# Five blocks of small products move into another PSUM pool, each directly beside a second set of small products

## The chip, the cores and the metric

The kernel runs on one core of a Trainium2 chip. The metric is the device time of one execution in microseconds. Five engines work side by side: PE (TensorE, matrix products), DVE (VectorE), ACT (ScalarE), POOL and SP (both used here to issue DMAs). Each engine takes its instructions strictly in the order in which the program was written; between engines, semaphores hold an instruction back until what it needs is there.

## The reference

Two branches over 2048 tokens of 512 channels are mixed by a gate for each token:

```python
g = sigmoid((x * gate_w).sum(-1, keepdims=True))
# branch a: a diagonal state space model as a long convolution
dt = exp(log_dt); A = -exp(log_A_real) + 1j * A_imag; C = (C_real + 1j * C_imag) * dt[:, None]
P = exp((A * dt[:, None])[:, :, None] * arange(2048))     # (512, 128, 2048)
K = 2.0 * einsum("dn,dnl->dl", C, P).real
a = irfft(rfft(u, 4096) * rfft(K, 4096))[:2048] + u * D_skip
# branch b: a bilinear gated unit, 512 -> 1792 -> 512
b = einsum("bsf,fd->bsd", (x @ w_gate) * (x @ w_up), w_down)
out = g * a + (1 - g) * b
```

## The kernel before

**Branch b** is most of PE's work. F = 1792 is cut into 14 slices, handled in four groups (3, 3, 4 and 4); for each group the four chunks of 512 tokens are gone through. `hidden` makes the products with the gate and the up weights in two PSUM banks, `pg` and `pu`, one bank each; `down` makes the products with the down weights in banks called `y`, of which there are two. To keep float32 accuracy with the fast float32r products, every operand is split into a high and a low part, and each product is three matmuls of 128x128 by 128x512 (called a *triple* below: `pg<-xs,wlo` once and `pg<-xs,whi` twice, or `y<-dhi,hl`, `y<-dlo,hh`, `y<-dhi,hh`). ACT copies `pg` to `h`, DVE multiplies `h` by `pu`, ACT and DVE split the result into `hh` and `hl`; ACT scales a finished `y` into `acc`, which is added to the output by a DMA.

**Branch a** makes the convolution kernel K in 16 blocks of 32 channels (`k_block(b, ...)`, b = 0 to 15). DVE and ACT build two tables of powers, `x` and `v`, and PE multiplies them: 64 small matmuls (128 rows by 32 columns of the array, 64 elements each) into one PSUM bank, `pk`. One ACT copy and two DVE operations take the bank into the tile `kt`. The transforms of u and of K, their products and the way back are further *sets of small products*, of other shapes, which take tiles of 32 or 64 rows of the array: `k<-in,w2s`, `k<-kt,w1k_t`, `k<-y,w3s`, `k<-in,w_t`. In the profile these small float32 products show as two records each. All of them, and `pk`, take banks called `k`, of which there are four (`bank()`). So PSUM's eight banks are: `y` two, `pg` and `pu` one each, `k` four.

**The order.** Every operation is first recorded as a task with an engine, a duration, and the tiles that it reads and writes (`Work.add`). `Work.plan` sorts the tasks with a model of the five engines, of the DMAs and of PE's instruction stream, and `Work.run` then writes them out in that order, after some of them have been moved by hand: a pair (n, other) in the table `AHEAD` puts task n directly before task other. This written order is the order on every engine. A PSUM or SBUF tile gets its buffer in the same order, in turn, and waits for the readers of the tile that had the buffer before.

On PE the sets of small products stand one at a time between the triples of branch b. All instructions are recorded through the helper class `InOrder`, so all carry one line in the profile (L124); tiles tell them apart.

Of the kernel before, what the change touches and what calls it, by code (L numbers as in the profile page):

```python
# [23 lines left out]
GROUPS = [range(0, 3), range(3, 6), range(6, 10), range(10, 14)]  # L24
SLOTS = max(map(len, GROUPS))
LAST = 3 if len(GROUPS) % 2 else 0
ROUND = 1.5 * 2.0**23
LN2_HI = 355.0 / 512.0
LN2_LO = math.log(2.0) - LN2_HI
# [86 lines left out]
class InOrder:  # L116


    def __init__(self, tc, engine):
        self.tc, self.engine, self.last = tc, engine, None  # L120
# [49 lines left out]
class Bus:  # L170
# [25 lines left out]
    def add(self, task, at, us):  # L196
        at = max(at, self.now)
        self.serve(self.queues, self.now, at)
        self.now = at
        self.queues[task.engine == "pool"].append([task, us])  # L200
        self.loads.append((at, sum(x[1] for q in self.queues for x in q)))
        return self.serve([[[*x] for x in q] for q in self.queues], at, 1e9)


class Work:
# [39 lines left out]
    SURE = {"pe": 3, "act": 2, "dve": 2}  # L245

    def __init__(self):
        self.tags, self.tasks = {}, []

    def tile(self, pool, tag, shape, dtype=F32, bufs=1, loose=False):  # L250
        return Tile(self, pool, tag, shape, dtype, bufs, loose)
# [189 lines left out]
            order.append(t)  # L441
        return order

    AHEAD = ((250, 57), (293, 292), (365, 364), (437, 436), (1140, 2246), (1149, 2246))

    def run(self):
        order = self.plan()
        at = {t.n: t for t in order}
        for n, other in self.AHEAD:
            order.remove(at[n])  # L450
            order.insert(order.index(at[other]), at[n])
            assert all(order.index(d) < order.index(at[n]) for d in at[n].deps)
        for t in order:
            t.fn()

# [2 lines left out]
def gated_mix_kernel(  # L458
# [19 lines left out]
    work = Work()  # L478
# [3 lines left out]
    def open_pool(name, bufs=1, space=None):  # L482
        kw = {} if space is None else {"space": space}
        return ctx.enter_context(tc.tile_pool(name=name, bufs=bufs, **kw))
# [9 lines left out]
    pools = {n: open_pool(n, b, PSUM) for n, b in (("ps_y", 2), ("ps_g", 1), ("ps_k", 4))}  # L494
# [3 lines left out]
    def new(pool, tag, shape, dtype=F32, bufs=1, loose=False):  # L498
        return work.tile(pools[pool], tag, shape, dtype, bufs, loose)

    def bank():
        return new("ps_k", "k", [P, D], bufs=4, loose=True)
# [5 lines left out]
    def stage(shape):  # L508
        return new("mid", "ts", shape, bufs=2, loose=True)
# [18 lines left out]
    def memsets():  # L528
        dve.memset(half_pi, math.pi / 2)
        dve.memset(shift, ROUND)  # L530
        dve.memset(skip, 0.0)
# [198 lines left out]
    def evacuate(gi, ci, r, y):  # L730
        t = 4 * ci + r
        final = gi == len(GROUPS) - 1 and ci == LAST
        if final and r > 1:
# [17 lines left out]
    def ends():  # L751

        t0 = 4 * LAST
        sums = new("tab", "kt", [P, 4, D])
# [4 lines left out]
        for r, acc in ending:  # L759
            t = t0 + r  # L760
            for q, (fin, parts) in late["fin"].items():
                add(
                    "dve", 0.25,
                    lambda r=r, q=q, t=t, fin=fin: dve.scalar_tensor_tensor(
                        sums.t[:, r, P * q : P * q + P], fin.t[:, 4 * (LAST % 2) + r], gate[:, t : t + 1],
                        sums.t[:, r, P * q : P * q + P], op0=ALU.mult, op1=ALU.add,
                    ),
                    r=[*parts, (m_gate, LAST)], w=[(sums, (r, 1))], rank=0,
                )
            for n, cs in enumerate((slice(0, D // 2), slice(D // 2, D)) if r == 3 else (slice(0, D),)):  # L770
# [7 lines left out]

                add("dve", 0.42 if r == 3 else 0.69, total, r=[acc, (m_gate, LAST)], w=part, rank=0)
                e, q = ("act", act) if n else ("sp", sp)  # L780
# [122 lines left out]
    def prologue():  # L903
# [23 lines left out]
        def exp(us, src, er, en, ep, ei, r, w, after=0.0):  # L927
# [9 lines left out]
            def ts(o, i, a, b, op0, op1=None):  # L937
                kw = {"op0": op0} if op1 is None else {"op0": op0, "op1": op1}
                op(0.62, "tensor_scalar", lambda: ((o(), i(), a, b), kw))

            def stt(o, i, a, j, op0, op1):
                op(1.0, "scalar_tensor_tensor", lambda: ((o(), i(), a, j()), {"op0": op0, "op1": op1}))

            ts(er, src, -87.0, 88.0, ALU.max, ALU.min)
            ts(en, er, 1.0 / math.log(2.0), ROUND, ALU.mult, ALU.add)
            ts(en, en, ROUND, None, ALU.subtract)
            stt(er, en, -LN2_HI, er, ALU.mult, ALU.add)
# [80 lines left out]
    def phases(b):  # L1028
# [7 lines left out]
            "dve", 0.85,  # L1036
            lambda: dve.scalar_tensor_tensor(t.t, rt.t, ROUND, t.t, op0=ALU.subtract, op1=ALU.subtract),
            r=[rt], w=[t],
# [132 lines left out]

    def k_block(b, x, v):
        pk = bank()

        def kgen():
            pv = pk.t.rearrange("p (g j) -> p g j", j=64)
            for g in range(TB // 4):
                for c in range(2):
                    for ch in range(4):
                        d = 4 * g + ch  # L1180
                        pe.matmul(
                            pv[32 * ch : 32 * ch + 32, g, :], x.t[:, c, d, :], v.t[:, c, d, :], start=c == 0, stop=c == 1,
                            tile_position=(0, 32 * ch),
                        )

        if b % 4 == 0:
            kts["now"] = new("tab", "kt", [P, 2, 2, 32, 16])
        kt, g0 = kts["now"], b % 4 * 8
        add("pe", 2.05, kgen, r=[x, v], w=[pk], rank=0, hold=[kt], count=256, slack=1.0)
        pv = lambda a: pk.t.rearrange("p (g a b k) -> p g a b k", a=2, b=2, k=16)[:, :, a]  # L1190
        side = lambda h: kt.t[:, h, :, g0 : g0 + 8].rearrange("p b g k -> p g b k")
        add("act", 0.37, lambda: act.copy(side(1), pv(0)[:, :, :, ::-1]), r=[pk], w=[(kt, (1, b % 4))])
        for h, op in enumerate((ALU.add, ALU.subtract)):
            add(
                "dve", 0.42, lambda h=h, op=op: dve.tensor_tensor(out=side(h), in0=pv(1), in1=side(1), op=op),
                r=[pk, (kt, (1, b % 4))], w=[(kt, (h, b % 4))], rank=0,
            )
        if b % 4 == 3:
            k_first(b // 4, kt)
# [196 lines left out]
    def m_last(q, gs):  # L1396

        banks, pieces, src = [[bank() for _ in range(2)] for _ in gs], [], []
        for g in gs:
# [6 lines left out]
            src.append(t)  # L1406
            cuts = ((1 - LAST % 2, 1), (LAST % 2, 1)) if q >= KT - 2 and g == LAST // 2 else ((0, 2),)
            to = t if q >= KT - 2 else stage([P, 8, P])
# [104 lines left out]
    for b in range(NB):  # L1513
        if b + 1 < NB:
            if b % 2 == 0:
                amplitudes([n for n in (b + 1, b + 2) if n < NB])
            phases(b + 1)
        v, old = v_table(b), x
        if b + 1 < NB:
            direct_powers(b + 1)  # L1520
            leads(b + 1)
            x = x_table(b + 1)
        k_block(b, old, v)
        if b % 4 == 3:
            transforms(b // 4)
# [56 lines left out]
```

## Time and profile before

| | |
|---|---|
| median of 3 runs | 579.96 us (579.47 to 580.79) |
| the profiled execution | 580.89 us |
| its span, from first to last instruction | 579.1 us |
| around the span | 1.8 us |
| PE, DVE, ACT, POOL busy in the span | 99%, 88%, 69%, 20% |
| DMA | 136.28 MB, mean 235 GB/s |
| granted TensorE clock | 1.0 in the whole span |

The profile is of one execution. Busy times are sums over the span, and a matmul's end is modelled, since matmuls overlap: the distance from one start to the next is the time that a matmul takes on PE. "PEld" are the weight loads that go with the matmuls. The queue "q8 instruction" among the DMA queues carries instruction code.

### The profile page before, as it was taken

The page shows a single profiled execution, that of the slowest core. Times are in us where ns is not written, and L with a number is a line of the kernel's source. Part 1 is how long each engine was busy: PE and PEld are TensorE (multiplying, and loading weights), DVE is VectorE, ACT ScalarE, POOL GpSimd, SP SyncE. Part 2 cuts the span into 40 slices and gives each one's busy share as a digit, 9 for nine tenths or more (in the row PEclk, how much of TensorE's full clock was granted, in tenths as well). Part 3 has the DMA queues.
Part 4 walks back from the last instruction along what each step waited for, and adds up shares of the span by engine and source line. Part 5 has one row for each costly group of instructions (what it writes and reads, how often), then busy time and mean ns, then how long its engine had stood idle before and what let it go on. Part 6 is the DMA issues. An engine that isn't in the chain of part 4 may idle for free.

```text
span 579.1 us, 14843 instructions
## 1 busy us (share of the span) xinstructions
PE 573.0 (99%) x5998; PEld 433.5 (75%) x5998; DVE 510.4 (88%) x812; ACT 401.4 (69%) x891; POOL 113.4 (20%) x159
## 2 busy tenths in 40 slices
PE   9999999999999999999999999999999999999997
PEld 5777777888886777788677868876778786776775
DVE  6999999999998999999999999997999996247555
ACT  5459888997579499968896775799887544243351
POOL 0003222312010240311032401103332103111011
PEclk9999999999999999999999999999999999999999
DMA  8999969998565797989679848978989349798986
GB/s 283 403 360 362 412 217 351 279 215 241 119 182 154 260 244 174 252 196 293 191 218 264 181 129 251 224 181 211 306 132 289 72 154 277 235 307 222 277 168 127
DMA packets 71687, 136.28 MB, mean 235 GB/s; under 512 B 6852, under 2 KB 35780, under 8 KB 69188
## 3 DMA queue, kind: packets, MB, share of 16 engines
q1 hardware_dynamic: 47668, 87.10, 43.3%
q0 software_dynamic: 23392, 47.98, 39.6%
q8 instruction: 47, 0.77, 0.5%
q10 hardware_dynamic: 560, 0.26, 0.2%
q14 instruction: 20, 0.16, 0.1%
HBM read 80.27 MB, written 55.05 MB: 234 GB/s over the span
## 4 chain that ended last, share of the span: by engine, by line
PE 94%; DMA 3%; ACT 1%; DVE 1%; issue 1%; DVEq 0%
PE pg L124 26%; PE y L124 26%; PE pu L124 26%; PE k L124 16%; DMA raw<-in_wts 2%; DMA y<-in_xT 1%; ACT ev L124 0%; ACT acc L124 0%; DVE dlo L124 0%; DVE t L124 0%; DVE v L124 0%; DVE sq L124 0%; ACT xs L124 0%; ACT v L124 0%; ACT h L124 0%
## 5 line engine op out<-in xcount | busy, mean ns | idle before, releaser
L124 PE MATMUL pg<-xs,whi 128*128 128x512 f32 x448 | 138.7, 391 | 0.2 <-ACT whi L124 0.2
L124 PE MATMUL pu<-xs,whi 128*128 128x512 f32 x448 | 138.3, 390 | 0.0
L124 PEld LDWEIGHTS pg<-xs,whi 128*128 128x128 f32 x448 | 84.1, 188 | 18.1 <-DVE xs L124 0.6
L124 PEld LDWEIGHTS pu<-xs,whi 128*128 128x128 f32 x448 | 84.1, 188 | 17.0
L124 PE MATMUL y<-dhi,hl 128*128 128x512 f32 x224 | 90.2, 403 | 0.1
L124 PE MATMUL pg<-xs,wlo 128*128 128x512 f32 x224 | 89.7, 400 | 0.5 <-ACT h L124 0.4
L124 PE MATMUL pu<-xs,wlo 128*128 128x512 f32 x224 | 89.4, 399 | 0.2 <-issue 0.2
L124 PE MATMUL y<-dlo,hh 128*128 128x512 f32 x224 | 87.7, 391 | 0.0
L124 PE MATMUL y<-dhi,hh 128*128 128x512 f32 x224 | 87.2, 389 | 0.0
L124 POOL DMA_DIRECT2D out<-acc x44 | 38.5, 929 | 171.0 <-ACT acc L124 170.4
L124 ACT COPY ev<-k 128x512 f32<-128x512 f32 x112 | 59.3, 598 | 14.8 <-PE k L124 12.3
L124 ACT CAST hh<-h 128x512 fp32r<-128x512 f32 x56 | 34.7, 620 | 44.6 <-DVE h L124 44.3
L124 DVE TENSOR_TENSOR h<-pu,h 128x512 f32<-128x512 f32 x56 | 38.5, 688 | 25.1 <-PE pu L124 22.5
L124 ACT ACTIVATE acc<-y,ngate 128x512 f32<-128x512 f32 x62 | 42.0, 688 | 24.3 <-PE y L124 22.8
L124 PEld LDWEIGHTS y<-dhi,hl 128*128 128x128 f32 x224 | 42.0, 188 | 21.0 <-issue 8.3
L124 PEld LDWEIGHTS pg<-xs,wlo 128*128 128x128 f32 x224 | 42.0, 188 | 20.1 <-issue 10.1
L124 PEld LDWEIGHTS pu<-xs,wlo 128*128 128x128 f32 x224 | 42.0, 188 | 17.2 <-issue 7.6
L124 ACT COPY h<-pg 128x512 f32<-128x512 f32 x56 | 33.0, 588 | 29.3 <-PE pg L124 24.6
L124 PEld LDWEIGHTS y<-dhi,hh 128*128 128x128 f32 x224 | 42.1, 188 | 9.0
L124 PEld LDWEIGHTS y<-dlo,hh 128*128 128x128 f32 x224 | 42.1, 188 | 8.1 <-issue 0.3
L124 DVE TENSOR_TENSOR hl<-h,hh 128x512 fp32r<-128x512 f32 x56 | 38.4, 687 | 3.6 <-ACT hh L124 3.1
L124 DVE TENSOR_TENSOR v<-m,v 128x896 f32<-128x896 f32 x32 | 34.1, 1085 | 0.2
(130 smaller groups left out, 959.2 us busy)
## 6 DMA issues: line engine op xcount, KB each, us to landing
xs<-xs_d SPq DMA_DIRECT2D x36, 512.0 KB, 6.0
out<-acc POOLq DMA_DIRECT2D x44, 256.0 KB, 6.0
raw<-in_wts SPq DMA_DIRECT2D x33, 256.0 KB, 4.8
xs_d<-xs SPq DMA_DIRECT2D x16, 512.0 KB, 7.8
su_d<-ev POOLq DMA_DIRECT2D x32, 256.0 KB, 6.1
y_d<-ts SPq DMA_DIRECT2D x28, 256.0 KB, 5.6
in<-su_d POOLq DMA_DIRECT2D x12, 512.0 KB, 7.2
sk_d<-ev SPq DMA_DIRECT2D x6, 1024.0 KB, 3.8
```

What stands on the lines that cost most here:

```text
L124: got = getattr(self.engine, name)(*args, **kw)
```

## The change

Five of the sixteen K blocks (0, 5, 8, 14 and 15) get their PSUM bank from the pool of the two `y` banks instead of the four `k` banks. The tile is planned as before, and takes its new home only when the order stands (`work.moved`). The table `AHEAD` grows, so that on PE each of these blocks stands directly beside another set of small products, with no triple between them; a few operations of ACT and DVE are moved with them. No operation is added or removed, and the orders on SP and POOL stay as they were.

```diff
+BESIDE = 0, 5, 8, 14, 15
...
-        self.tags, self.tasks = {}, []
+        self.tags, self.tasks, self.moved = {}, [], []
...
-    AHEAD = ((250, 57), (293, 292), (365, 364), (437, 436), (1140, 2246), (1149, 2246))
+    AHEAD = (
+        (250, 57), (293, 292), (365, 364), (437, 436),
+        (444, 167), (1485, 445), (170, 451), (171, 451), (1490, 451),
...
+    )
...
-            assert all(order.index(d) < order.index(at[n]) for d in at[n].deps)
+        self.checked(order)
+        for tile, home in self.moved:
+            tile.pool, tile.tag, tile.bufs = home
         for t in order:
             t.fn()
...
     def k_block(b, x, v):
         pk = bank()
+        if b in BESIDE:
+            work.moved.append((pk, (pools["ps_y"], "y", 2)))
```

(`checked` goes through the order and asserts that every task stands behind those that it depends on.)

On PE, around K block 0, before the change (the names carry buffer numbers; `k_1155<-in` is the last of a set of the first transform of u, `k_1193<-v` the K block, `pg` and `pu` are triples):

```order
L124 MATMUL k_1155<-in_875,w2s_164 64x512
L124 MATMUL pg_1143<-xs_944,wlo_214 128x512
L124 MATMUL pg_1143<-xs_944,whi_204 128x512 x2
L124 MATMUL pg_1143<-xs_950,wlo_214 128x512
L124 MATMUL pg_1143<-xs_950,whi_204 128x512 x2
L124 MATMUL pg_1143<-xs_1055,wlo_214 128x512
L124 MATMUL pg_1143<-xs_1055,whi_204 128x512 x2
L124 MATMUL k_1193<-v_752,x_458 32x64 x64
L124 MATMUL pu_1273<-xs_679,wlo_214 128x512
```

And after it:

```order
L126 MATMUL pg_1143<-xs_944,whi_204 128x512 x2
L126 MATMUL k_1152<-in_875,w2s_164 64x512
L126 MATMUL k_1154<-in_875,w2s_164 64x512
L126 MATMUL k_1156<-in_875,w2s_164 64x512
L126 MATMUL k_1158<-in_875,w2s_164 64x512
L126 MATMUL y_1176<-v_752,x_458 32x64 x64
L126 MATMUL pg_1143<-xs_950,wlo_214 128x512
L126 MATMUL pg_1143<-xs_950,whi_204 128x512 x2
L126 MATMUL pg_1143<-xs_1055,wlo_214 128x512
L126 MATMUL pg_1143<-xs_1055,whi_204 128x512 x2
L126 MATMUL pu_1273<-xs_679,wlo_214 128x512
```

The set of the transform stands one triple later, and the K block two triples earlier, now in a `y` bank. K blocks 5 and 8 come to stand behind such a set in the same way (two triples and six triples earlier), and block 14 keeps its place while the set behind it comes three triples earlier.

On PE, around K block 15, before the change (`k_6278<-v` is the K block; the set `k_6225` to `k_6231` that will stand beside it is four triples ahead):

```order
L124 MATMUL y_6205<-dhi_5447,hl_6185 128x512
L124 MATMUL y_6205<-dlo_5468,hh_6183 128x512
L124 MATMUL y_6205<-dhi_5447,hh_6183 128x512
L124 MATMUL pg_6265<-xs_5656,wlo_4868 128x512
L124 MATMUL pg_6265<-xs_5656,whi_4850 128x512 x2
L124 MATMUL y_6272<-dhi_5281,hl_5891 128x512
L124 MATMUL y_6272<-dlo_5294,hh_5882 128x512
L124 MATMUL y_6272<-dhi_5281,hh_5882 128x512
L124 MATMUL k_6278<-v_752,x_5763 32x64 x64
```

And after it (`y_6272` is now the K block's bank, `y_6337` the sums that were `y_6272`):

```order
L126 MATMUL pg_6231<-xs_5656,whi_4850 128x512 x2
L126 MATMUL k_6235<-in_5593,w2s_5591 32x512
L126 MATMUL k_6237<-in_5593,w2s_5591 32x512
L126 MATMUL k_6239<-in_5593,w2s_5591 32x512
L126 MATMUL k_6241<-in_5593,w2s_5591 32x512
L126 MATMUL y_6272<-v_752,x_5763 32x64 x64
L126 MATMUL y_6337<-dhi_5281,hl_5891 128x512
```

The set moved three triples later, the K block one triple earlier, and the K block takes a `y` bank in turn between two pairs of sums.

On ACT, where K block 12 is taken out of its bank (it keeps a `k` bank), before the change (`ts` is scaled by the gate in two halves, `dhi<-raw` is the high part of down weights that a DMA brings, `h<-pg` empties the bank `pg`):

```order
L124 ACTIVATE ts_5267<-ts_5267,gate_83 128x128 x8
L124 ACTIVATE ts_5276<-ts_5276,gate_83 128x128 x8
L124 CAST dhi_5433<-raw_5303 128x512
L124 CAST hh_5439<-h_5322 128x512
L124 COPY x_5445<-pb_4184 128x64
L124 CAST dhi_5447<-raw_5309 128x512
L124 COPY kt_5455<-k_5324 128x8x2x16
L124 COPY h_5459<-pg_5423 128x512
```

And after it:

```order
L126 ACTIVATE ts_5267<-ts_5267,gate_83 128x128 x8
L126 COPY kt_5411<-k_5324 128x8x2x16
L126 ACTIVATE ts_5276<-ts_5276,gate_83 128x128 x8
L126 CAST dhi_5437<-raw_5303 128x512
L126 CAST hh_5443<-h_5322 128x512
L126 COPY x_5451<-pb_4184 128x64
L126 COPY h_5453<-pg_5425 128x512
L126 CAST dhi_5455<-raw_5309 128x512
```

The copy of the K block comes ahead of eight operations of the scaling, and the second `dhi<-raw` stands behind `h<-pg` instead of ahead of it.

More of the change, by code (lines that the diff above doesn't have):

```diff
@@ L442, in plan, with checked @@
         return order
-    AHEAD = ((250, 57), (293, 292), (365, 364), (437, 436), (1140, 2246), (1149, 2246))
+    AHEAD = (
[8 rows of a table added]
+    )
+    @staticmethod
+    def checked(order):
+        done = set()
+        for t in order:
+            assert t.deps <= done
+            done.add(t)
     def run(self):
```

6 rows, old and new, of the table AHEAD are left out of this document.

## The prediction

> **What bounds the kernel now.** I read the page first (busy shares, chain, queues), then PE's waits, then PE's timeline at the five places, then DVE and ACT there, and last the fetches of instruction code. The page:
>
> ```profile
> span 579.1 us, 14843 instructions
> ...
> PE 573.0 (99%) x5998; PEld 433.5 (75%) x5998; DVE 510.4 (88%) x812; ACT 401.4 (69%) x891; POOL 113.4 (20%) x159
> ...
> q8 instruction: 47, 0.77, 0.5%
> ...
> PE 94%; DMA 3%; ACT 1%; DVE 1%; issue 1%; DVEq 0%
> ```
>
> PE is busy 99% of the span and carries 94% of the chain that ended last. PE's waits hold little, and these two are the ones far inside the span (at 420 and at 382):
>
> ```profile
> PE pg L124 <- ACT h L124: 0.4, 1, 0.4
> ...
> PE pu L124 <- issue: 0.2, 1, 0.2
> ```
>
> So what PE saves is saved, and what holds PE is lost, nearly everywhere. The busy share hides what a set of small products costs beside its own work. The timeline of PE around K block 5 (start, duration, engine, instruction, count) shows it:
>
> ```profile
> 215.63 0.39 PE L124 MATMUL pu<-xs,wlo 128*128 128x512 f32 x1
> ...
> 216.40 1.14 PE L124 MATMUL k<-in,w2s 32*32 32x512 f32 x32
> 217.47 0.50 PE L124 MATMUL pu<-xs,wlo 128*128 128x512 f32 x1
> ...
> 218.27 0.40 PE L124 MATMUL pg<-xs,wlo 128*128 128x512 f32 x1
> ...
> 218.96 0.39 PE L124 MATMUL pg<-xs,wlo 128*128 128x512 f32 x1
> ...
> 219.73 1.99 PE L124 MATMUL k<-v,x 128*32 128x64 f32 x128
> 221.66 0.50 PE L124 MATMUL pg<-xs,wlo 128*128 128x512 f32 x1
> ...
> 222.46 0.40 PE L124 MATMUL pg<-xs,wlo 128*128 128x512 f32 x1
> ```
>
> A triple takes 0.68 (three starts 0.227 apart). After the triple at 215.63 the next start would be 216.31; the set comes at 216.40, 0.09 late. The triple behind the set lasts 217.47 to 218.27, 0.80, 0.12 over. The K set pays the same: 218.96 + 0.68 = 219.64 against 219.73, and 221.66 to 222.46. A visit to small products so costs 0.21 us beside its work.
>
> **The change, part by part.** *Five visits fewer.* Two sets side by side pay one entry and one return instead of two. No trace row shows two sets of different shapes meeting. If PE passes from one to the other as it now passes to a triple, 0.21 is saved; if the meeting costs another entry, 0.12; if the second set slips in without the 0.09, 0.30. I take 0.21, since entry (0.09) and the wait at a set's end look alike for all shapes of set here. The Trainium skill, "TensorEngine Tiling (Array Packing)", Key Properties, says that changing the tiling mode drains the array; no run here shows it between two small modes; by it the end 0.30 falls away.
>
> *Inputs and banks.* A K block that moves forward needs `x` and `v` sooner. At block 0 the last write of `v` on DVE, and PE's timeline:
>
> ```profile
> 95.89 0.66 DVE L124 TENSOR_TENSOR v<-v,sq 128x256 f32<-128x256 f32 x1
> ```
>
> ```profile
> 94.54 0.39 PE L124 MATMUL pg<-xs,wlo 128*128 128x512 f32 x1
> ...
> 95.31 1.11 PE L124 MATMUL k<-in,w2s 32*64 32x512 f32 x16
> 96.35 0.50 PE L124 MATMUL pg<-xs,wlo 128*128 128x512 f32 x1
> ...
> 98.61 2.17 PE L124 MATMUL k<-v,x 128*32 128x64 f32 x128
> 100.72 0.50 PE L124 MATMUL pu<-xs,wlo 128*128 128x512 f32 x1
> ```
>
> The set now starts a triple later, 95.99, and takes 96.35 - 95.31 = 1.04, so block 0 starts at 97.03, 0.5 after `v` (96.55). Block 15 has the least room (PE, DVE, ACT):
>
> ```profile
> 478.45 1.14 PE L124 MATMUL k<-in,w2s 32*32 32x512 f32 x32
> ...
> 482.46 1.99 PE L124 MATMUL k<-v,x 128*32 128x64 f32 x128
> ```
>
> ```profile
> 480.18 0.62 DVE L124 TENSOR_TENSOR v<-v,sq 128x256 f32<-128x256 f32 x1
> ```
>
> ```profile
> 480.52 1.38 ACT L124 ACTIVATE acc<-y,ngate 128x512 f32<-128x512 f32 x2
> ```
>
> Block 15 starts a triple and the set's saved 0.21 + 0.12 earlier, near 481.4 to 481.6; `v` is written at 480.80, and the `y` bank that it takes is emptied by the first of two `acc` at about 481.2, or 0.5 sooner since one `ev` copy no longer stands ahead of it. Its own bank is wanted again by the second pair of sums, 12 matmuls or 2.72 after its end, while the copy and the two DVE operations follow within 2. I cost this at nothing; if the cover fails, PE waits some 0.3 there. At the other four places the next `y` comes later still. Queues: SP and POOL keep their orders; the transform sets at blocks 0, 5 and 15 end 0.7 to 2 later, so their stores or loads go out that much later, and nothing on PE reads them for several us.
>
> *The wait at 420.* ACT and PE before:
>
> ```profile
> 410.50 4.79 ACT L124 ACTIVATE ts<-ts,gate 128x128 f32<-128x128 f32 x16
> ...
> 416.84 0.31 ACT L124 COPY x<-pb 128x64 f32<-128x64 f32 x1
> 418.68 0.62 ACT L124 CAST dhi<-raw 128x512 fp32r<-128x512 f32 x1 [1.53 <-DMA raw<-in_wts]
> 419.21 0.36 ACT L124 COPY kt<-k 128x256 f32<-128x256 f32 x1
> 419.47 0.59 ACT L124 COPY h<-pg 128x512 f32<-128x512 f32 x1
> ```
>
> ```profile
> 419.10 0.61 PE L124 MATMUL pu<-xs,whi 128*128 128x512 f32 x2
> 420.11 0.50 PE L124 MATMUL pg<-xs,wlo 128*128 128x512 f32 x1 [0.40 <-ACT h L124]
> ...
> 420.91 0.40 PE L124 MATMUL pg<-xs,wlo 128*128 128x512 f32 x1
> ```
>
> ACT stands 1.53 before a cast whose weights are still on their way; behind it are K block 12's copy and `h<-pg`, for which PE waits: two matmuls from 419.10 end the slot at 419.55, PE goes on at 420.11 and its first triple takes 0.80: 0.56 + 0.12 = 0.68. With the cast behind `h<-pg`, the copy can run from 417.2, as soon as `pg` is done (four `pu` triples ahead of 419.55, so 416.8), and ends at 417.8, 1.7 before PE asks. Late next are the second cast and the `dlo` that follows it on DVE, for sums that stand behind the following products; DVE's two operations of K block 12 move ahead of them. Gain 0.68, 0 where the weights land sooner anyway. At blocks 0 and 8 `h<-pg` is moved among ACT's work too; there the bank is wanted again four triples (2.72) after its product ends, and ahead of the copy stand at most eight scalings (half of the 4.79 above): nothing.
>
> *The code of block 0.* Block 0's set shows 2.17 where all later ones show 1.99: 0.18 inside it. Where, and why, the counts of records up to four moments tell (window, us, then PE and PEld with their counts):
>
> ```profile
> 0.00:88.97 88.97, 87.59 (x443) 63.52 (x443) 82.56 (x168) 63.37 (x145) 13.98 (x49) 1.00 0.92 341
> 0.00:98.61 98.61, 97.23 (x494) 70.36 (x494) 91.96 (x183) 72.06 (x161) 16.11 (x53) 1.00 0.93 344
> 0.00:100.21 100.21, 98.83 (x601) 71.95 (x601) 93.49 (x187) 73.66 (x165) 17.03 (x54) 1.00 0.93 342
> 0.00:382.26 382.26, 380.69 (x3900) 291.36 (x3900) 365.43 (x588) 295.71 (x664) 74.20 (x119) 1.00 0.86 249
> ```
>
> The DMA queues in the window 98.0 to 99.1, PE's timeline at 382, and the group of the K sets' records:
>
> ```profile
> q8 instruction: 1, 0.02, 5.5%
> ```
>
> ```profile
> 382.27 0.50 PE L124 MATMUL pu<-xs,wlo 128*128 128x512 f32 x1 [0.20 <-issue]
> ```
>
> ```profile
> L124 PE MATMUL k<-v,x 128*32 128x64 f32 x2048 | 32.1, 220 | 0.0
> ```
>
> The page's q8 has 47 packets in 0.77 MB, 16 KB each, and 11,996 records stand in PE's stream: some 256 instructions a packet. At 100.21 PE had begun 601 matmuls and 601 loads; with the 15 semaphore waits of the built program that is 1217. At 382.26, where PE idles with no releaser ("issue"), it is 7800 + 73 = 7873, exactly 26 times 256 further. So both holds stand at the border of a code packet. The one packet between 98.0 and 99.1 took 5.5% of 16 engines in 1.1 us, 0.97 us, and its code ran at about 100.2. The trace's packets start 1 to 9 us after the stream comes within 64 instructions of the packet ahead; here that was at 88.97 (886 records), ahead of every moved instruction, and the queues that then held it up were filled ahead of them too. So I expect it no sooner than before. But PE now reaches the border sooner: in the changed program instruction 1217 is the 113th of block 0's 128 records, at 97.03 + 112 x 0.014 = 98.6 (0.014: 1.99 less a record's 0.22, over 127 steps). PE then stands from 98.6 to 100.2: 1.6. Behind it: 15 records (0.21) and the set's end (219.73 to 221.66 less 127 steps, 0.15), so a triple starts at 100.6, the return's 0.12, and two triples (1.36) that stood ahead of the set before: the `pu` product begins at 102.1, against 100.72 + 0.12 with its return paid. Net +1.24, with the 0.21 and the 0.18 inside it. Ends: -0.39 when the packet is there in time, +1.7 when it comes 0.5 later. I take +1.24, since the profile gives the arrival.
>
> *Sum*, against the profiled execution (580.89, of which the span is 579.1): blocks 5, 8, 14, 15: 4 x -0.21 = -0.84; wait at 420: -0.68; block 0: +1.24. Together -0.28, or 580.6. That execution lies 0.93 above the median of the runs; on the median 579.7.
>
> **The rivals.** *A: the code is there in time* in the timed runs. Then block 0 gives -0.39 and the sum is -0.84 - 0.68 - 0.39 = -1.9: 578.0. For it: the hold was only 0.18 of a set's time, and the runs between 579.47 and 580.79 say that some holds come and go. Against it: the same border held PE in the profile although PE came 1.5 later than it will. The Trainium skill, "Runtime: NRT & Kernel Launch", Instruction fetch mechanics, has the code streamed in 16 KiB blocks of 256 instructions and calls the cost of a border mostly hidden; the packets agree (47, 0.77 MB), "hidden" fails at 100.2 and 382.3, and by it A would hold.
>
> *B: the wait at 420 stays*, because the weights land sooner in the timed runs and there was little to gain, or `h` is held by something else: -0.84 + 1.24 = +0.4: 580.4, no measurable change.
>
> *C: slower.* Block 15 has a border too: instruction 10177, the 94th of its records, is now reached 1 us sooner (482.7 for 483.7), and its packet was on its way between 480.7 and 481.7 (the same q8 row in that window); used 1.2 later, as the one of block 0 was, it holds PE for 0.2 at most. If it is as late as block 0's, PE stands 1.6 there, and the sum is +1.3: 581.3, slower. It decides from about 1.5 us of further hold.
>
> **How the numbers follow.** What the measurement can tell from no change is about 0.2%, 1.16 us. The forecast, block 0 held with the other terms as summed: 0.47, at 579.7, own range 578.9 to 580.5. A: 0.32. B: 0.10. C: 0.11. Faster by over 0.2%: A nearly whole, 0.29, and the forecast's cases with a hold below 0.7, 0.06: 0.35. Slower: C and 0.01 of B: 0.12. The rest, 0.53, within. Range: from A to short of C, 577.8 to 580.8.
>
> **What would show it.** In the changed profile: the five places with no triple between the sets; at block 0 one row of far more than 2 us for its 128 records (about 3.5) when I am right, 1.8 to 2.0 under A; PE going on at 420 with no wait for ACT; DVE and ACT busy as before. I am wrong if block 0's row is short, or if PE shows new waits on DVE or ACT at blocks 8, 14 or 15.

## The result, and the profile after

The changed kernel took 582.62 us (median of 13 runs, 581.19 to 587.03); the kernel before, on the same chips, 580.66 (578.83 to 582.18). The ratio is 1.0053, 95% interval 1.0035 to 1.0072: slower by half a percent, where 579.7 was forecast. The profiled execution took 581.19, the least of the 13, so its trace shows the least of what went wrong; a second profile was taken for that (below).

The page of the changed kernel, and two of PE's waits:

```profile
span 579.4 us, 14830 instructions
...
PE 571.7 (99%) x5998; PEld 434.4 (75%) x5998; DVE 510.9 (88%) x812; ACT 400.9 (69%) x891; POOL 113.4 (20%) x159
...
PE 90%; DVE 7%; DMA 1%; ACT 1%; issue 1%; DVEq 0%; ACTq 0%
```

```profile
PE y L126 <- issue: 1.6, 2, 1.0
...
PE y L126 <- ACT acc L126: 0.3, 1, 0.3
```

The work is the same; DVE now carries 7% of the chain, where it had 1%, and `y <- issue` and `y <- acc` are new. PE's profile alone doesn't say where the time went. That is told by the 2016 matmuls of its triples, which come in the same order in all kernels. The table gives, for stretches between matmuls of the same number, how much longer (+) or shorter PE took than in the profiled execution before; the times at the head are those of before.

```
                    start  block0 block5 block8 334-   382   wait   bl.14 block15  sum with
                    -95    95-110 216-33 291-06 350          at 420       465-498  the rest
changed             +0.17  +0.87  -0.33  -0.22  +0.49  -0.52 -0.75  -0.20 +0.95    +0.42
changed, again      +0.17  +2.01  -0.39  -0.22  +1.41  -0.52 -0.75  -0.21 +0.99    +2.31
no 0                +0.19  +0.02  -0.39  -0.22  +2.86  -0.21 -0.75  -0.21 +0.04    +1.15
no 15               -0.00  +0.92  -0.39  -0.22  +3.41  -0.52 -0.75  -0.21 +0.69    +2.75
no 0, no 15         +0.95  +0.27  -0.39  -0.22  +0.03  +0.21 -0.75  -0.21 +0.46    +0.18
no 8                +0.16  -0.22  -0.39   0.00  -0.01  -0.52 -0.75  -0.21 +1.33    -0.82
8 alone             +0.10  -0.01  -0.13  -0.22  +1.22  +0.35 -0.75   0.00 -0.02    +0.47
5, 14               +0.19  +0.51  -0.33   0.00  +0.04  -0.35 -0.75  -0.20 +0.40    -0.63
5, 14, 15           +0.16  +0.42  -0.39   0.00  -0.01  -0.16 -0.75  -0.21 -0.01    -1.16
5, 14, 15, again    +0.03  -0.01  -0.39   0.00  -0.01  -0.18 -0.75  -0.21 +0.04    -1.69
before, again       +0.54  +0.25  -0.01   0.00  -0.01  -0.13 +0.01   0.00 -0.03    +0.41
```

Three places lose and vary from run to run: block 0, the stretch 334 to 350, where nothing was moved, and block 15. The stretch at 382 and the first 95 us vary too, as they do between the two profiles of before; the other stretches are steady.

*The small gain is there.* PE at block 5 after the change, set and K block side by side:

```profile
218.13 1.14 PE L126 MATMUL k<-in,w2s 32*32 32x512 f32 x32
219.20 2.01 PE L126 MATMUL y<-v,x 128*32 128x64 f32 x128
221.14 0.50 PE L126 MATMUL pg<-xs,wlo 128*128 128x512 f32 x1
```

*Block 0* is held inside, after 113 of its 128 records:

```profile
96.16 1.11 PE L126 MATMUL k<-in,w2s 32*64 32x512 f32 x16
97.20 1.81 PE L126 MATMUL y<-v,x 128*32 128x64 f32 x113
100.05 0.43 PE L126 MATMUL y<-v,x 128*32 128x64 f32 x15 [1.04 <-issue]
100.41 0.50 PE L126 MATMUL pg<-xs,wlo 128*128 128x512 f32 x1
```

*Block 15* is held twice, before its first record and after the 94th; the rows are PE, ACT and DVE:

```profile
480.07 1.14 PE L126 MATMUL k<-in,w2s 32*32 32x512 f32 x32
481.50 1.54 PE L126 MATMUL y<-v,x 128*32 128x64 f32 x94 [0.28 <-ACT acc L126]
483.56 0.75 PE L126 MATMUL y<-v,x 128*32 128x64 f32 x34 [0.53 <-issue]
```

```profile
480.22 1.25 ACT L126 ACTIVATE acc<-y,ngate 128x512 f32<-128x512 f32 x2
```

```profile
480.51 0.83 DVE L126 TENSOR_TENSOR v<-v,sq 128x256 f32<-128x256 f32 x1
```

The bank is free only when the second `acc` ends (481.47), and `v` comes at 481.34, 0.54 later than before.

*334 to 350* is the end of a chain that begins on POOL at block 8. POOL before, and after:

```profile
293.12 1.85 POOL L124 DMA_DIRECT2D in<-su_d  x2 [12.75 <-PE k L124]
295.33 0.89 POOL L124 DMA_DIRECT2D in<-sk_d  x1 [0.36 <-issue]
298.38 0.88 POOL L124 DMA_DIRECT2D in<-sk_d  x1 [2.17 <-issue]
301.90 1.58 POOL L124 DMA_DIRECT2D out<-ts  x1 [2.64 <-DVE x L124]
308.29 1.56 POOL L124 DMA_DIRECT2D out<-ts  x1 [4.82 <-issue]
...
320.78 2.75 POOL L124 DMA_DIRECT2D out<-acc  x3
```

```profile
294.61 1.85 POOL L126 DMA_DIRECT2D in<-su_d  x2 [13.15 <-PE k L126]
296.44 0.90 POOL L126 DMA_DIRECT2D in<-sk_d  x1
301.13 0.88 POOL L126 DMA_DIRECT2D in<-sk_d  x1 [3.80 <-issue]
304.58 1.58 POOL L126 DMA_DIRECT2D out<-ts  x1 [2.57 <-ACT v L126]
314.49 1.56 POOL L126 DMA_DIRECT2D out<-ts  x1 [8.33 <-ACT sq L126]
...
324.52 2.75 POOL L126 DMA_DIRECT2D out<-acc  x3
```

PE is 0.81 later there than before, and the set stands a triple (0.68) later, so the loads start 1.49 later; the second `in<-sk_d` is 2.75 later, the second `out<-ts` 6.20, and the stores `out<-acc` 3.74. How long the first `in<-su_d` and the first `out<-ts` took to land (the last column, us; first the two of before, then those of after):

```profile
in<-su_d POOLq DMA_DIRECT2D x1, 512.0 KB, 4.9
out<-ts POOLq DMA_DIRECT2D x1, 512.0 KB, 6.1
```

```profile
in<-su_d POOLq DMA_DIRECT2D x1, 512.0 KB, 6.1
out<-ts POOLq DMA_DIRECT2D x1, 512.0 KB, 9.6
```

The second `in<-sk_d` goes out 0.4 after the first load has landed, and the second `out<-ts` 0.3 after the first has, in all twenty profiles of this study; the first `out<-ts` goes out 0.3 after the first `in<-sk_d` has landed (8.46 after the first load went out before, 9.66 after). The releasers that the rows name (`v`, `sq`) are only the last that moved.

The store itself, the first `out<-ts`, is the larger part of the delay, and here the view of the queues shows what it shared the 16 DMA engines with while it was under way (301.90 to 307.98 before, 304.58 to 314.17 after; packets, MB, share of the engines):

```profile
q0 software_dynamic: 1098, 0.70, 83.1%
q1 hardware_dynamic: 63, 0.26, 12.9%
```

```profile
q0 software_dynamic: 1062, 0.57, 52.8%
q1 hardware_dynamic: 379, 1.42, 39.9%
q8 instruction: 1, 0.02, 0.8%
```

POOL's queue (q0) took 5.1 us of all engines both times, 83.1% of 6.08 and 52.8% of 9.59. SP's queue (q1) took 0.8 before and 3.8 after, 3.0 of the 3.5 by which the store was longer. What SP issued beside it are four loads of 512 KB, `xs<-xs_d`. The first of them went out 12.29 after POOL's first load before, and 11.39 after it in the changed kernel: the set, behind which POOL's loads stand, is a triple later (0.68), and PE behind it has saved the 0.22 of block 8's visit.

ACT then wants a buffer of `acc` that such a store must empty. ACT at 330 before, after, and in the kernel without block 15, where it was worst; below it, in that kernel, what stood behind it on ACT, DVE and PE:

```profile
329.57 0.69 ACT L124 ACTIVATE acc<-y,ngate 128x512 f32<-128x512 f32 x1
```

```profile
331.19 0.69 ACT L126 ACTIVATE acc<-y,ngate 128x512 f32<-128x512 f32 x1 [0.92 <-DMA out<-acc]
```

```profile
333.79 0.69 ACT L126 ACTIVATE acc<-y,ngate 128x512 f32<-128x512 f32 x1 [3.81 <-DMA out<-acc]
...
336.59 0.36 ACT L126 COPY kt<-k 128x256 f32<-128x256 f32 x1
```

```profile
336.99 0.42 DVE L126 TENSOR_TENSOR kt<-k,kt 128x256 f32<-128x256 f32 x1 [2.98 <-ACT kt L126]
```

```profile
338.49 2.04 PE L126 MATMUL k<-y,w3s 32*64 32x128 f32 x122 [1.86 <-DVE kt L126]
```

PE's set at 338 needs a bank that DVE's `kt` empties, and the set at 346 takes banks while ACT, late too, still copies them out: with block 8 alone moved it took 2.26 where it took 1.14 before. In the six profiles with the full move of block 8, `acc` waited 0.92, 1.82, 3.30, 3.81, 0.44 and 1.65 (in the order of the table), and PE lost 0.49, 1.41, 2.86, 3.41, 0.03 and 1.22: each time the wait less 0.4.

### The profile page after: what moved, and what is told of

Its sections match the earlier page's. It is cut to its first block, busy times and chain, and to the rows that moved or that the text cites. A ratio compares the mean times of both kernels' runs of the same rounds, so it can differ in the third digit from the quotient of the medians.

```text
span 579.4 us, 14830 instructions
## 1 busy us (share of the span) xinstructions
PE 571.7 (99%) x5998; PEld 434.4 (75%) x5998; DVE 510.9 (88%) x812; ACT 400.9 (69%) x891; POOL 113.4 (20%) x159
## 4 chain that ended last, share of the span: by engine, by line
PE 90%; DVE 7%; DMA 1%; ACT 1%; issue 1%; DVEq 0%; ACTq 0%
PE y L126 26%; PE pg L126 25%; PE pu L126 25%; PE k L126 14%; DVE v L126 2%; DVE x L126 1%; DMA y<-in_xT 1%; DVE m L126 1%; DVE y L126 1%; DVE h L126 0%; DVE hl L126 0%; DVE ev L126 0%; ACT acc L126 0%; DVE kt L126 0%; DVE ri L126 0%
## 5 line engine op out<-in xcount | busy, mean ns | idle before, releaser
L126 ACT COPY ev<-k 128x512 f32<-128x512 f32 x112 | 59.3, 598 | 14.4 <-PE k L126 11.8
```

What stands on the lines that cost most here:

```text
L126: got = getattr(self.engine, name)(*args, **kw)
```

## The experiments

Each kernel is the changed one with some of its five blocks put back (its number out of `BESIDE`, its line out of `AHEAD`), if no other edit is shown.

**Which block loses.** First, block 0 put back:

```diff
-BESIDE = 0, 5, 8, 14, 15
+BESIDE = 5, 8, 14, 15
...
-        (444, 167), (1485, 445), (170, 451), (171, 451), (1490, 451),
```

> The changed kernel, but K block 0 stays where it was and in its k bank (blocks 5, 8, 14, 15 and the ACT and DVE moves at 420 stay). Theory 1 (the loss sits in the two merged visits of blocks 0 and 15, where PE stands for instruction code and, at 15, for its bank): block 0's visits cost the two old ones again, 3.58 instead of 4.47, so this kernel lies 0.9 below the changed one in the profile and 1 to 2 below its median of 582.6: ratio to before 1.001 to 1.003. Theory 2 (the loss is spread over later borders of code packets or later waits, and block 0's hold is taken back): same median as the changed kernel, 1.005.

Measured 581.77 (578.72 to 585.43), ratio 1.003 (1.001 to 1.0051). Block 0's loss is gone (+0.02), but 334 to 350 cost 2.86: a place that neither theory named.

Block 15 put back (`BESIDE = 0, 5, 8, 14`, and the two lines of block 15 out):

> The changed kernel, but K block 15 stays where it was and in its k bank (blocks 0, 5, 8, 14 and the moves at 420 stay). Theory 1: block 15's visits cost 3.43 again instead of 4.37, so 0.9 below the changed kernel in the profile and 1 to 2 below its median: ratio 1.001 to 1.003; block 0 still shows its hold of about 1.3 at the code border. Theory 2: 1.005 as the changed kernel, and PE stands elsewhere behind 484.

Measured 583.86 (580.86 to 589.67), 1.0055 (1.0034 to 1.0076): 1.4 below the changed kernel on the same chip (585.21, below), as theory 1 had it, but far over the ratio that theory 1 gave, since 3.41 went at 334 to 350.

Both put back:

> The changed kernel with neither block 0 nor block 15 moved: blocks 5, 8 and 14 (each 0.20 to 0.22 less in the profile) and the moves at 420 (0.67 less). Theory 1: 1.3 below before, ratio 0.997 to 0.999. Theory 2: still above 1.002, with long runs as the changed kernel has them (up to 587), since the loss does not sit in those two places.

Measured 580.92, 1.0024 (1.0008 to 1.0039). With the two holds gone a loss is left; theory 1 is not enough.

No edit:

> The changed kernel itself once more, for a second profile and more times. Theory 1: the median again near 582.6 and ratio 1.003 to 1.007; holds at block 0 and block 15 of the profile again, at the same instructions, with other lengths (0.5 to 3). Theory 2: the holds are at other places than in the first profile.

Measured 585.21 (583.12 to 586.37), 1.0085 (1.0066 to 1.0105), above what theory 1 gave. The same instructions hold PE, for other lengths; block 0:

```profile
97.21 1.81 PE L126 MATMUL y<-v,x 128*32 128x64 f32 x113
101.15 0.43 PE L126 MATMUL y<-v,x 128*32 128x64 f32 x15 [2.14 <-issue]
```

From these profiles came the chain from POOL's loads (theory S), tried next. Block 8 put back:

> The changed kernel, but K block 8 stays where it was and in its k bank, with the set beside it, its two loads and the scaling of ts as before. Theory S (stores): at block 8 the set k<-in,w4_t stands a triple later, POOL's loads after it go out 0.7 later, each further issue on POOL waits for an earlier transfer, the second out<-ts comes 6 later (314.5 for 308.3), the out<-acc behind it 4 later, ACT's acc at 330 waits for its buffer (0.4 to 3.8 in the profiles), and behind it stand kt, hence PE's set at 338, and the tables x and v. So here the second out<-ts is back at 308 to 309.5 (in before's time), acc at 330 waits under 0.2, PE loses nothing between 334 and 350, block 15 does not wait for v or acc. The sum by the profile: blocks 5 and 14 -0.4, the wait at 420 -0.67, block 0 +0.9, block 15 +0.5 (its code border alone): +0.3, ratio 1.000 to 1.002, and 2 to 3 below the changed kernel's median on the same chip. Rival B (banks: the turns of y and k that the change gave all later tiles): still 1.004 or more, with the same wait at 330.

Measured 581.57 (580.05 to 583.4), 1.0015 (1.0004 to 1.0027). As theory S said, `acc` at 330 doesn't wait, 334 to 350 costs nothing (-0.01), and the long runs are gone. Its last claim failed: block 15 still waits for its bank, and the code border there costs more (+1.33 for the block). Block 0's packet was in time here and the whole 0.22 came out:

```profile
97.19 2.18 PE L126 MATMUL y<-v,x 128*32 128x64 f32 x128
...
479.94 1.54 PE L126 MATMUL y<-v,x 128*32 128x64 f32 x94 [0.33 <-ACT acc L126]
482.34 0.74 PE L126 MATMUL y<-v,x 128*32 128x64 f32 x34 [0.86 <-issue]
```

Block 8 alone, in the kernel before (`BESIDE = 8,` and its line of `AHEAD`):

> The kernel before with K block 8 alone moved beside its set (its three moves, y bank). Theory S: PE saves 0.22 at block 8, and loses 0.4 to 3.4 between 334 and 350, from run to run: acc at 330 waits 0.4 to 4 for out<-acc, second out<-ts at 313 to 316. Ratio 1.001 to 1.005, with a spread of several us. Rival B: 0.9995, no wait at 330.

Measured 581.91 (579.32 to 584.64), 1.0025 (1.0008 to 1.0042): block 8 alone makes a loss, the wait at 330 (1.65) and the spread. Rival B, which had 0.9995 and no wait, falls.

Blocks 5 and 14 with the moves at 420:

> Only blocks 5 and 14 and the moves at 420; blocks 0, 8 and 15 as before. Theory S: blocks 5 and 14 -0.4 and the wait at 420 -0.67 come out whole: 1.1 below before, ratio 0.9975 to 0.999, spread as before. Rival B: 1.001 or more.

Measured 580.02 (579.14 to 580.76), 0.999 (0.998 to 1.0): as expected in direction, half in size. Its profile loses 0.51 at block 0 and 0.40 at block 15, neither of which was moved here.

Block 8 a triple further forward, so that the set keeps its place (blocks 0 and 15 put back as well):

```diff
-        (888, 1693), (1996, 893), (1697, 901),
+        (1996, 888), (1697, 901),
```

> Blocks 5, 8, 14 and the moves at 420, but at block 8 the set k<-in,w4_t keeps its old place and K block 8 comes a triple further forward, to stand directly behind it. It differs from the kernel without blocks 0 and 15 (1.0024) by that one triple. Theory S: second out<-ts at 308 to 309.5, acc at 330 waits under 0.2, PE loses nothing at 334 to 350; 1.3 below before, ratio 0.997 to 0.999. Rival B: 1.002 as that kernel.

Measured 581.13 (580.19 to 582.88), 1.0011 (0.9999 to 1.0023), between the two expectations. 334 to 350 cost 0.10, but the second `out<-ts` still came late, 17.98 after the first load for 15.17 before. So the set's lateness is not all. This profile also loses 0.69 between 291 and 334, where PE waits for `h` (0.20, at 303.65) and for `acc` (0.12, at 318): the 0.22 of the visit didn't come out.

**What makes POOL's chain late.** The set alone a triple later, in the kernel before:

```diff
+    AHEAD = (..., (888, 1693), (1140, 2246), (1149, 2246))
```

> The kernel before with one triple of PE put ahead of the set k<-in,w4_t at block 8, so that the set stands 0.68 later, and nothing else: K block 8 keeps its place and its k bank. PE's own work is the same. Theory S (stores): this alone makes the loss: second out<-ts at 313 to 316 (308.3 before), acc at 330 waits 0.4 to 4, PE loses 0.5 to 3.4 between 334 and 350; ratio 1.001 to 1.005 and a spread of several us. Rival B (the y bank or the place of K block 8): ratio 1.000, second out<-ts at 308 to 310.

Measured 580.41, 1.0007 (0.9996 to 1.0019): theory S as put here fell. Second `in<-sk_d` 5.38 after the first load, second `out<-ts` 15.63, nothing lost at 334 to 350. Two things went with the loss in all profiles: where the code packet of border 21 lay (the 22nd of the 47, counted from 0), and where SP's first `xs<-xs_d` lay against the first `out<-ts`, by the trace's records. Times are after the first `in<-su_d`; the fifth column is how long that store took:

```
                                      packet   second    first out<-ts       first      second      PE lost
                                      starts   in<-sk_d  out       took      xs<-xs_d   out<-ts     334-350
block 8 not moved (10 profiles)       7.2-8.0  5.2-5.4   8.7-9.5   6.1-6.5   12.3 (a)   15.2-16.1   0.0
block 8 and its set moved (6)         2.8-3.6  6.3-6.8   9.7-10.2  9.6-11.5  11.4       19.9-21.8   0.03-3.41
block 8 moved, set in place (1)       3.7      6.4       9.9       7.8       12.6       18.0        0.10
block 8 three triples earlier (1)     7.7      5.2       9.5       6.3       12.3       16.2        0.0
30 copies ahead of block 7 (1)        1.5      5.6       9.1       6.2       12.3       15.6        0.0
14 copies ahead of blocks 1 to 7 (1)  5.8      5.4       10.2      6.6       12.3       17.1        0.0
(a) 11.6 with the set alone moved
```

A K block is 256 instructions, a packet's worth. Moved 6 triples forward it brings PE to border 21 some 4.7 earlier, beside POOL's loads, and the packet (0.9 to 1.2 long) is then under way while their data come. They land later (6.1 for 4.9 in the rows above), and the first `out<-ts` goes out 1.2 later. There it meets SP's loads, which in the six come 0.9 sooner, and takes 9.6 to 11.5: SP's queue moved 1.4 to 2.1 MB beside it in the six, 0.8 with the set in place, and 0.2 to 0.5 in the other thirteen. Neither shift did it alone: with the set alone late, SP's loads came early (11.6) but the store too (9.0), and it took 6.4; with the 14 copies the store came late (10.2) but SP's loads too (12.3), and it took 6.6. The packet of border 22 (11.6 to 11.8 in the six) also falls beside the store, but took under 1% of the engines' time there. No run moved SP's loads by themselves, so this rests on the order of events in the twenty profiles. The last three rows are the attempts to part the packet from the block:

Copies of a product in K block 7 of the kernel before, to shift the borders:

```diff
+                    if b == 7 and g + c == 0:
+                        for _ in range(30):
+                            pe.matmul(pv[0:32, 0, :], x.t[:, 0, 0, :], v.t[:, 0, 0, :], start=True, stop=True, tile_position=(0, 0))
```

> The kernel before, with 30 further copies of K block 7's first small product ahead of it (they write what that product writes again): 0.8 of PE's time, and 120 instructions that put every later border of a code packet 120 instructions earlier in the work. No block and no set is moved. PE then comes within 64 of border 21 at about 293.5 + 0.8 instead of 298.56. Theory P (code packets among the loads): the packet then starts 2.5 to 4 after the first in<-su_d, as in the six kernels with block 8 moved, instead of 7.5 to 8; the second in<-sk_d goes out 6.2 to 6.8 after that load instead of 5.2 to 5.4, the second out<-ts 17.5 to 22 after it instead of 15.2 to 15.7, acc at 330 waits up to 4, and PE loses up to 3 between 334 and 350: ratio 1.002 to 1.006, with a spread of several us. Rival M (it is the place of K block 8 itself, its bank, or ACT's and DVE's order around it): 5.2 to 5.4 and 15.2 to 15.7 stay, and the ratio is 1.0014 by the copies alone.

Measured 589.31, 1.0157 (1.0141 to 1.0172). Inconclusive: PE stood for code inside the longer block, and the packet came at 1.54, ahead of the loads' data. The loads were hardly later (5.62), as such a place allows, but that isn't the test.

The control, the same copies with `b == 10`:

> The control: the same 30 copies ahead of K block 10 (near 351), behind the loads in question. Theory P and rival M alike: second in<-sk_d 5.2 to 5.4, second out<-ts 15.2 to 15.7 after the first load; the copies alone give 1.0014; later borders shift, so holds may come or go there (1.0005 to 1.0025).

Measured 585.17, 1.0095 (1.0081 to 1.0109); POOL's times as before (5.33 and 15.55). The copies cost 3.3, not 0.8: 0.11 each.

Two copies each in the K blocks 1 to 7 (`b in range(1, 8)`, `range(2)`):

> The kernel before, with two further copies of the first small product ahead of each of the K blocks 1 to 7 (14 in all, 0.4 of PE's time), which put every border from block 8 on 56 instructions earlier in the work. No block and no set is moved. PE then comes within 64 of border 21 some 0.5 to 1 after the first in<-su_d, as with block 8 moved (0.72 to 0.78), instead of 4.8 to 5.4. Theory P: the packet starts 2.8 to 3.7 after that load, the second in<-sk_d goes out 6.2 to 6.8 after it instead of 5.2 to 5.4, the second out<-ts 17.5 to 22 after it instead of 15.2 to 16.1, acc at 330 waits; ratio 1.002 to 1.006 with a spread of several us. Rival M (the place of K block 8 itself): 5.2 to 5.4 and 15.2 to 16.1 stay, ratio 1.0007 by the copies.

Measured 583.01, 1.0046 (1.0031 to 1.006), in the profile all from the copies and from holds elsewhere; 334 to 350 lost nothing. The packet came at 5.84, again not where it was wanted. With it among the later loads the first `out<-ts` went out at 10.18 (8.7 to 9.5 without block 8's move) and the second at 17.14. So POOL's stores came late though block 8 stood still, against rival M; the `in<-sk_d` of theory P did not.

Block 8 three triples forward, in the kernel before:

```diff
+    AHEAD = (..., (1140, 2246), (1149, 2246), (1996, 896))
```

> The kernel before with K block 8 alone moved, three triples earlier (half of the change's way), in its k bank, the set where it was. PE comes within 64 of border 21 at 3.2 to 3.5 after the first in<-su_d. Theory P: the packet starts at 5 to 6.5, when the first load has landed: second in<-sk_d at 5.2 to 5.5 as before, second out<-ts at 15 to 17, acc at 330 waits under 1, ratio 0.9995 to 1.001. Rival M: half of the delay, 5.8 and 17 to 18, ratio 1.001 to 1.002.

Measured 581.5, 1.0022 (1.0014 to 1.0031). The packet started at 7.66, later than expected, and POOL kept its times (5.22, 16.18), as theory P has it and rival M has not. The ratio is above both expectations, though its interval reaches into rival M's (1.001 to 1.002): this profile loses 0.99 between 306 and 334, where PE waits for `acc`, and 0.59 at 382.

**Single terms.** The moves at 420 alone (`BESIDE = ()`, the fourth line of `AHEAD`):

> The kernel before with the moves of ACT and DVE around 420 alone; no K block moved. If the wait at 420 stands in most runs as in the profile of before, this gains 0.67 of 580: ratio 0.9988, at most 0.9995. If the wait is there in some runs only, since the weights land at another time from run to run, 0.9995 to 1.0005.

Measured 580.13, 0.9998 (0.999 to 1.0007), though its profile shows the wait gone (-0.75).

> The kernel before itself, for a second profile. The moves at 420 alone gave 0.9998 though the profile of before shows a wait of 0.67 there: if that wait is there in some runs only, this profile shows 0 to 0.3 at 420; if it is there in all, 0.5 to 0.8 again, and what took its gain is to be looked for elsewhere. Ratio 1.000.

Measured 579.96, 1.0 (0.9992 to 1.0009). The profile shows the wait again (+0.01 against the first). But it took 581.46, the longest of its 11 runs, as the first profile lay 0.93 over its median.

Block 0 and its set behind the second `pu` triple, with 5, 14 and 420:

```diff
+        (167, 449), (1485, 449), (168, 449), (169, 449), (170, 449), (171, 449),
+        (172, 449), (173, 449), (1486, 449), (1495, 449),
```

> Blocks 5 and 14 and the moves at 420, and block 0 beside its set as well, but with both behind the second pu triple (the set five triples later than before, K block 0 two). The border of the code packet is then the 102nd of block 0's records and PE comes to it near 101.3, where the packets of the profiles so far let it go on between 98.95 and 101.5. Theory code: no step inside block 0 over 0.1, so its visit saves 0.2, and the hold of 0.1 to 0.6 that the unmoved block showed in five of six profiles is gone: 0.2 to 0.7 below the kernel with blocks 5 and 14 alone, ratio 0.998 to 0.999. Rival (PE stands there for data of block 0, or because y holds the bank): a hold inside or ahead of block 0 stays, 1.000 or more.

Measured 583.92, 1.0061 (1.0046 to 1.0076), far above both expectations. Inside block 0 the theory holds: its code is there, and no step is long. But ACT's copies, moved with the set, stand ahead of others, PE waits 0.35 and 0.60 for `h` and `hl` (106.7, 113.7), and 1.9 go at block 15.

```profile
100.03 1.99 PE L126 MATMUL y<-v,x 128*32 128x64 f32 x128
106.68 0.50 PE L126 MATMUL pu<-xs,wlo 128*128 128x512 f32 x1 [0.35 <-DVE h L126]
113.69 0.50 PE L126 MATMUL y<-dhi,hl 128*128 128x512 f32 x1 [0.60 <-DVE hl L126]
```

Blocks 5, 14 and 15 with the moves at 420:

> Blocks 5, 14 and 15 and the moves at 420; blocks 0 and 8 as before. Block 15's own price against the kernel with blocks 5 and 14 alone (0.999): the visit saves 0.2, the wait for its bank or for v costs 0.2 to 0.5 (theory S: less, since the tables are not late here, but acc still holds the bank to the end of its second sum), the code border 0.6 to 1.1 less the 0.4 that PE loses there without the move. Together +0.2 to +0.9: ratio 0.9995 to 1.0005. Rival: the merged visit comes out with its 0.2, ratio 0.9985.

Measured 579.61 (578.98 to 580.83), 0.9989 (0.9976 to 1.0002). The interval reaches into both expectations; the profile is with the rival, since the stretch of block 15 took 0.41 less than with blocks 5 and 14 alone, and 0.01 less than before. Block 15 waits a little for its bank, and its code is in time:

```profile
480.78 1.99 PE L126 MATMUL y<-v,x 128*32 128x64 f32 x128 [0.17 <-ACT acc L126]
```

> Blocks 5, 14 and 15 and the moves at 420 once more, for a second profile and more times (0.9989, 0.9976 to 1.0002 the first time). If blocks 0 and 8 carry the whole loss: 0.998 to 0.9995 again, block 15 without a step over 0.1 inside it or with one of at most 0.5.

Measured 579.59 (578.63 to 581.02), 0.9995 (0.9985 to 1.0005). Both give the lowest medians of the study; neither can be told from before. So blocks 0 and 8 carry the loss: without both it is gone, with either it is there (1.0015 without 8, 1.003 without 0). No run moved block 0 alone in the way of the change.

## Why the prediction was wrong, by its own steps

- *Five visits fewer, 0.21 each.* Right. Blocks 8 and 14 gave 0.22 and 0.20; block 5 gave 0.33 to 0.39, of which 0.18 is a stall at 229.75 that was gone in kernels without a moved block 5 as well.
- *Queues: "SP and POOL keep their orders"; the sets at blocks 0, 5 and 15 end later, and nothing reads them for several us.* This is the first of two steps that failed. It left out block 8, whose set also stands a triple later, with POOL's loads behind it; and it looked only at which product reads them, not at POOL's queue or at the loads of SP's queue that its stores meet. The real chain is load, `out<-ts`, next `out<-ts`, `out<-acc`, `acc`'s buffer on ACT, `kt`, PE. It cost 0.03 to 3.41 (mean of six 1.57) against a saving of 0.22. That block 8 makes it is shown (1.0025 alone; 1.0015 without it, against 1.0053 and 1.0085 with it), that a late set alone does not, too. That the code packet lengthens the loads, and SP's loads the store, is not isolated: it rests on where they lay in twenty profiles, and on the block moved half the way. No run put the packet among the first loads without the block, none moved SP's loads, and none moved block 8 the whole way in its `k` bank, so that its new bank stays a rival.
- *The code of block 0: net +1.24, ends -0.39 and +1.7.* Right in kind, the size varies: +0.87, +2.01, +0.92, and -0.22 with the code in time. Wherever the border held PE it went on 1.2 to 1.6 after the packet had landed (97.6 to 99.6 in these four), at the border's record. One profile's arrival was taken for the middle; it is one draw, and the upper end was too low. The Trainium skill, "Runtime: NRT & Kernel Launch", Instruction fetch mechanics, calls the cost of a border mostly hidden; most of the 47 show no step here, but the one inside block 0 held PE by 1.0 to 2.1 in three of four profiles.
- *Block 15's inputs: nothing, or 0.3.* The second step that failed, and in the first profile the larger miss (+0.95 where -0.21 was summed). The bank was taken for free after the first `acc`; it is free after the second, and PE waited 0.17 to 0.33 for it, in the changed kernel's second profile 0.46 for `v`. The border, to which rival C gave 0.2 at most, held PE by 0.6 to 1.1 in three profiles. Together the stretch lost 0.95 to 1.33 where block 0 was moved too, and nothing in three profiles where it was not. What links the two isn't settled; the packet of block 15 started 0.1 to 0.4 ahead of the block's first record in the former, and 1.2 to 1.9 ahead in the latter. Part of the loss isn't block 15's: with block 14 moved and block 15 in place the stretch lost 0.40 to 0.69 as well (no 15; no 0, no 15; 5, 14), in two of the three since the next pair of sums waits for the `y` bank at 481. So the 0.20 of block 14 was paid back there in these kernels, and came out whole in the three that moved block 15 and not block 0.
- *The wait at 420: -0.68.* Right in every profile with the moves (-0.75), but the moves alone gave 0.9998, and why the median didn't gain is open. Without the moves the wait comes and goes: against before, PE took 0.75 less there in three kernels that don't have them (8 alone, block 8 three triples earlier, 30 copies ahead of block 7), 0.46 and 0.36 less in two, 0.01 more in the repeat, and 0.35 more in another. The weights' load landed 10.84 us after it went out before and 10.85 in the repeat, 9.69 with block 8 alone moved, and 11.80 in the kernel that lost more. Rival B, that the weights land sooner, so holds in some kernels; that the wait differs between runs of the same kernel is not shown, since both profiles of before have it, and both are of long runs.
- *Sum and range.* -0.28 was worked out; the two profiles gave +0.42 and +2.31, and the median lies higher. That the first is so near is in part luck: it holds -0.52 at 382, a code border that was priced in no term. The range added up uncertain prices of one execution, and had nothing for a wait that grows from run to run.

## What to carry to other kernels

Where a product moves, follow each transfer behind it down its queue to the next buffer that somebody waits for, not only to the reader of its data: here loads that landed 1.2 us later put a store beside another queue's loads, which made the next store 6 late and another engine wait up to 3.8. Moving a dense set of small instructions moves the code fetches too, and their packets pass through the same 16 DMA engines. Price a hold that depends on a transfer's arrival from several profiles, and look whether the profiled run lies high or low among its times.

## What was not expected of the hardware

- POOL's fourth load of 512 KB went out only 0.4 us after the first had landed, in all twenty profiles, though the semaphore that it names had been up for long (since 284.1 before, where the load went out at 298.4).
- Copies of a small product into the same place cost 0.11 us each (3.3 for 30), two records of 0.056, where the products of a K block step by 0.014 a record. The factor is four, as many as the tiles of the array that the block's products take in turn, where the copies keep to one; the two were not tried apart.
- After PE had stood 2.8 us for code (kernel with 30 copies in block 7), the granted clock fell to half for 3.4 us. Each row has the stretch, PE's busy time and count, the granted clock, the DMA share and GB/s:

```profile
280.00:283.00 3.00, 0.44 (x14) 1.00 0.31 64
283.00:284.00 1.00, 1.00 (x4) 0.86 0.00 0
284.00:287.00 3.00, 3.00 (x8) 0.50 0.00 0
```
